# Filler matmuls moved to another PSUM bank, and loads of right sides pinned behind the output weights, in a fused attention and two-MoE kernel

## The chip, the cores and the metric

The kernel runs on one core of one Trainium2 chip. The metric is the device time of one execution in microseconds, smaller is better. A core has a matmul engine (TensorE, PE in the profile), a vector engine (DVE), a scalar engine (ACT), GpSimd (POOL) and a sync engine (SP). SP computes nothing here: nearly all DMAs are issued from its queue, in the order in which they stand there, and an issue that has to wait holds up every issue behind it.

## The reference

```python
def _attn_ref(q, k, v, tau):                      # (4, 8, 576, 64) each
    scores = scale * np.matmul(q, k.transpose(0, 1, 3, 2))
    thresh = np.max(scores, axis=-1, keepdims=True) - tau
    scores = np.where(scores >= thresh, scores, -1000000000.0)
    scores = scores - np.max(scores, axis=-1, keepdims=True)
    attn = np.exp(scores)
    attn = attn / (np.sum(attn, axis=-1, keepdims=True) + 1e-09)
    return np.matmul(attn, v)

def _moe_ref(x, w_in, w_out, s, b):               # x (2304, 512), w_in (512, 2048)
    r = np.maximum(x @ w_in, 0.0)
    return (s * (r * r) + b) @ w_out

def _moe2_ref(x, w_in, w_out):
    h = x @ w_in
    g = h * np.tanh(np.where(h > 20.0, h, np.log1p(np.exp(np.minimum(h, 20.0)))))
    return g @ w_out
```

The attention output, laid out as 2304 rows of 512, goes through the first layer pair (`_moe_ref`) and then the second (`_moe2_ref`).

## The kernel before

All large matmuls work on float32 split into two parts (high and low), so a product of two matrices is three matmuls.

**Attention.** The 32 heads are taken as 16 pairs `pr`; each pair has 9 score tiles `ti` of 128 rows by 576 columns, and the loop in `attention` counts them as `k = 9 * pr + ti`. For a tile, `scores` writes S into PSUM in two halves of 288 columns (line 318), one half in each bank of a two-bank tile. In the first three pairs it then writes two filler matmuls (`busy`, line 179: ones times ones, a result that nobody uses) into columns 800 to 1023 of the same tile (line 320). The fillers keep the matmul engine occupied. DVE then reads S (`ns`, line 324), ACT takes the exponential (line 331), DVE masks and sums (line 335), POOL normalizes (line 345). Seven tiles later `weights_t` transposes the weights into the PSUM tile `T` (lines 357 to 366) and ACT copies them out (`te`, line 368); `product` multiplies them with the values into the PSUM tile `pv` (line 379). The right order of all this is found by a scheduler that simulates a time line when the kernel is built, so the program's order on an engine isn't the order of the code.

PSUM has eight banks, and in the first stage four two-bank tiles fill them: two for S (also used for the transposed q and k, `tp`), one for `T`, one for `pv`. The transposed k of the next pair is made in tile 2 of a pair, q in tile 4: `raw_t` transposes, ACT copies the high part (`hik`, `hiq`, line 258), DVE subtracts (`lok`, `loq`, line 259), SP moves the parts into place (`KH`, line 279). The high part has one buffer, so `hiq` waits until `hik` has been moved.

Before the first tile, 16 wider fillers run in a tile called `warm`, which lies in the bank of `T` (lines 411 to 413).

**First layer pair.** `moe1` is interleaved with the attention from the time the first four pairs are there.

**Second layer pair.** `moe2` takes three blocks `sb` of 768 rows, with Strassen's scheme: seven products p = 1, 6, 5, 2, 7, 3, 4 in place of eight. For a block, `hidden` runs over j = 0 to 7; for each j it needs 7 weight parts in two tiles, `wi{sb}_{j}_0` (parts 6, 5, 1; 768 KB) and `wi{sb}_{j}_3` (parts 2, 4, 7, 3; 1024 KB), and seven right sides `yc{sb}_{p}`. A product is 6 matmuls (line 587). Then `output` runs over p = 1, 6, 2, 7, 5, 4, 3, each with 72 matmuls (line 721) and two weight tiles `wo{sb}_{p}_{q}` of 1024 KB (line 715). All `wi` and `wo` tiles share one ring of five buffers (`wr`): each load waits until the tile five places before it is done with. At the end of each p the output stage also asks for the right side of the same p for the next block (line 727), which the hidden stage has by then done with, and after the last three products and p = 2 it stores output tiles (line 671). The right sides of the next block are computed during `hidden` and stored to DRAM as `ycd` (line 559).

Of the kernel before, what the change touches and what calls it, by code (L numbers as in the profile page):

```python
# [8 lines left out]
F32 = mybir.dt.float32  # L9
# [6 lines left out]
P = 128  # L16
# [3 lines left out]
class Fused:  # L20
# [281 lines left out]
    def scores(self, pr, ti):  # L302
        nc = self.nc
        Q, KH, KL, E4 = self.sets[pr % 2]
        if ti == 0:
            self.st = self.at.tile([P, 5, 9], F32, tag="stat", name=f"st{pr}", bufs=2)
        st = self.st
        nm, nthr, sm, u, rinv = (st[:, i, :] for i in range(5))
        hs = [0] if ti < 4 else [1] if ti > 4 else [0, 1]
        cols = slice(512, 640) if ti == 4 else slice((ti % 5) * 128, (ti % 5) * 128 + 128)  # L310
        S = self.s_tile(f"S{pr}_{ti}")
        for hf in range(2):
            ks = slice(hf * 288, hf * 288 + 288)
            so = S[:, hf * HB:hf * HB + 288]
            terms = [(h, K[h]) for h in hs for K in (KH, KL)]
            for i, (h, kt) in enumerate(terms):
                c0 = ti * 128 + 64 * h if ti <= 4 else 64 + ti * 128
                nc.tensor.matmul(so, Q[:, c0:c0 + 128], kt[:, ks], start=(i == 0), stop=(i == len(terms) - 1))  # L318
        if pr < 3:
            self.busy(S[:, 800:1024], 2)  # L320
        ns = self.at.tile([P, 576], F32, tag="ns", name=f"ns{pr}_{ti}", bufs=2)
        sv = S.rearrange("p (h n) -> p h n", h=2)[:, :, :288]
        c1 = slice(ti, ti + 1)
        nc.vector.tensor_scalar(ns.rearrange("p (h n) -> p h n", h=2), sv, -0.125, 3.0e38,  # L324
                                op0=ALU.mult, op1=ALU.min, accum_out=nm[:, c1])
        nc.gpsimd.tensor_scalar(nthr[:, c1], nm[:, c1], self.tau_c, None, op0=ALU.add)  # L326

        if ti < 4:
            self.es[pr, ti, "pair"] = self.at.tile([P, 1152], F32, tag="e", name=f"e{pr}_{ti}", bufs=8)
        e = E4[:, 64:640] if ti == 4 else self.es[pr, ti % 5, "pair"][:, 0 if ti < 4 else 576:][:, :576]  # L330
        nc.scalar.activation(e, ns, AF.Exp, bias=nm[:, c1], scale=-1.0)  # L331
        self.es[pr, ti] = e

        def finish():
            nc.vector.scalar_tensor_tensor(e, ns, nthr[:, c1], e, op0=ALU.is_le, op1=ALU.mult, accum_out=sm[:, c1])  # L335
            if ti not in (1, 4, 8):
                return
            g = slice({1: 0, 4: 2, 8: 5}[ti], ti + 1)
            nc.vector.tensor_scalar(rinv[:, g], sm[:, g], 1.0e-9, None, op0=ALU.add)
            nc.vector.reciprocal(rinv[:, g], rinv[:, g])  # L340

            nc.vector.tensor_scalar(u[:, g], sm[:, g], 0.5, 1.0 / self.S, op0=ALU.is_lt, op1=ALU.mult)
            for j in range(g.start, g.stop):
                t = self.es[pr, j]
                nc.gpsimd.tensor_scalar(t, t, rinv[:, j:j + 1], u[:, j:j + 1], op0=ALU.mult, op1=ALU.add)  # L345

        return finish
# [49 lines left out]
    def attention(self):  # L397

        nc = self.nc
        N = 9 * self.B * self.NP
        LAG = 7
        for n in "kq":
            self.load_raw(0, n)
        nc.sync.dma_start(self.tau_c, self.tau.partition_broadcast(P))
        nc.sync.dma_start(self.s_c, self.s.partition_broadcast(P))
        nc.sync.dma_start(self.b_c, self.b.partition_broadcast(P))
        for pr in range(2):
            self.load_raw(pr, "v")  # L410
        warm = self.tp.tile([P, 1024], F32, tag="T", name="warm")
        self.busy(warm[:, :512], 10)
        self.prep_first(lambda n: self.busy(warm[:, :512], n))
        fin = todo = None
        tes = {}
        for k in range(N + LAG + 2):
            pr, ti = divmod(k, 9)
            if k < N:
                nxt = self.scores(pr, ti)
                if fin:  # L420
                    fin()
                fin = nxt
                yield 550
                if pr + 1 < self.B * self.NP and ti in (2, 4):
                    self.prep_qk(pr + 1, "kq"[ti // 2 - 1])
                    yield 500
            elif fin:
                fin()
                fin = None
            j = k - LAG  # L430
            if 0 <= j < N:
                prj, ci = divmod(j, 9)
                tnew = self.weights_t(prj, ci)
                yield 550
            if todo:
                tp, tc, te = todo
                tes[tc] = te
                if tc == 4:
                    self.product(tp, 4, (te, te), True, False)
                    yield 490  # L440
                elif tc > 4:
                    self.product(tp, tc - 5, (tes[tc - 5], te), False, tc == 8)
                    yield 970
                if tc == 8:
                    self.split_x(tp)
                    self.load_raw(tp + 2, "v")
            todo = (prj, ci, tnew) if 0 <= j < N else None
# [187 lines left out]
    def output(self, sb):  # L635
        nc = self.nc
# [69 lines left out]
        def run():  # L706
            for i, (p, q) in enumerate(seq):
# [16 lines left out]
                            after(p, t)  # L724
                if sb < 2 and q == 3:
                    t = self.yc[p] = self.ycp.tile([P, 2, 2, N2], F32R, tag=f"yc{p}", name=f"yc{sb + 1}_{p}")
                    nc.sync.dma_start(t.bitcast(F32), self.ycd[p])

        return prep, run

# [179 lines left out]
```

## Time and profile before

| what | value |
|---|---|
| three timed runs | 1165.19, 1164.51, 1174.03 us; median 1165.19 us |
| the profiled execution | 1174.32 us, of which the span of its instructions is 1172.3 us |
| PE busy | 1110.8 us (95% of the span) |
| mean granted TensorE clock | 0.983 |
| DMA | 292.71 MB, mean 250 GB/s |
| PE time in `output` (line 721) | 180.6 us, idle before it 5.3 us |

The profile is of one execution. Busy time of PE says only that a matmul was in the pipe. The granted clock is 1.00 where the engine runs at 2.4 GHz and 0.50 where it runs at 1.2 GHz; a figure between is a mean over a stretch that has both.

### The profile page before, as it was taken

The numbers are of one execution on the slowest core, as the hardware profiler recorded it, in microseconds if no ns is written. First come the engines' busy times: TensorE is split into PE (matmuls) and PEld (weight loads), VectorE is DVE, ScalarE is ACT, GpSimd is POOL, SyncE is SP. The second block draws the span as 40 slices with busy tenths as digits, with TensorE's granted clock in tenths as the row PEclk, the third lists the DMA queues.
The fourth block names the chain that finished last, engine by engine and source line by source line (L and its number), as shares of the span: only waits on it lengthen the run. The fifth ranks groups of instructions, "written<-read, shape, count | busy, mean of one in ns | idle before, by whom it ended". The sixth has DMA issues, their size and how long they took to land.

```text
span 1172.3 us, 21473 instructions
## 1 busy us (share of the span) xinstructions
PE 1110.8 (95%) x7966; PEld 1022.7 (87%) x7966; DVE 760.7 (65%) x1516; ACT 616.5 (53%) x1153; POOL 421.1 (36%) x536
## 2 busy tenths in 40 slices
PE   7888999998989989999899999999998999999998
PEld 5766788787788878888799889999998999999998
DVE  5678766869687575767676515573786368734783
ACT  4456675746557555557565447563453144513451
POOL 4457656658456565638475323310000000000000
PEclk8899999899999999999999999999998999999999
DMA  6347665675778778798876249998999899987783
GB/s 157 72 100 209 163 185 169 201 215 182 231 243 268 239 225 266 250 273 262 273 234 201 86 135 327 380 352 316 367 371 372 285 401 349 419 274 255 266 293 121
DMA packets 141592, 292.71 MB, mean 250 GB/s; under 512 B 52848, under 2 KB 78960, under 8 KB 133168
## 3 DMA queue, kind: packets, MB, share of 16 engines
q1 hardware_dynamic: 134256, 286.91, 73.1%
q10 hardware_dynamic: 7232, 4.43, 1.5%
q8 instruction: 63, 1.03, 0.4%
q14 instruction: 41, 0.34, 0.1%
HBM read 201.85 MB, written 66.58 MB: 229 GB/s over the span
## 4 chain that ended last, share of the span: by engine, by line
PE 55%; DMA 16%; DVE 12%; POOL 5%; ACT 5%; issue 5%; SPq 2%; ACTq 0%; DVEq 0%; POOLq 0%
PE o L721 13%; PE y L476 10%; PE h L476 8%; PE qY L587 6%; PE qX L587 4%; PE qV L587 4%; PE pv L379 4%; DVE e L335 3%; PE S L318 3%; DMA wo<-wso 3%; DMA crawi<-in_moe_w_in_dram 2%; POOL e L345 2%; PE T L357 2%; DMA wso<-chlo 2%; DMA wraw<-in_moe_w_in_dram 2%
## 5 line engine op out<-in xcount | busy, mean ns | idle before, releaser
L721 PE MATMUL o<-wo,hl 128*128 128x256 f32 x1512 | 180.6, 282 | 5.3 <-DMA wo<-wso 5.3
L721 PEld LDWEIGHTS o<-wo,hl 128*128 128x128 f32 x1512 | 180.1, 190 | 5.6 <-issue 3.6
L476 PE MATMUL y<-gh,w 128*128 128x288 f32 x768 | 165.2, 301 | 3.7 <-ACT y L521 2.4
L476 PE MATMUL h<-xh,w 128*128 128x288 f32 x768 | 163.9, 299 | 4.5 <-ACT r L497 2.1
L335 DVE SCALAR_TENSOR_TENSOR e<-ns,st,e 128x576 f32<-128x576 f32 x128 | 123.6, 970 | 61.6 <-ACT e L331 40.4
L324 DVE TENSOR_SCALAR_CACHE_REDUCE ns<-S 128x576 f32<-128x576 f32 x144 | 107.8, 753 | 58.1 <-PE S L318 46.8
L345 POOL TENSOR_SCALAR e<-e,st 128x576 f32<-128x576 f32 x128 | 133.1, 1049 | 32.8 <-DVE st L340 26.0
L476 PEld LDWEIGHTS y<-gh,w 128*128 128x128 f32 x768 | 126.9, 190 | 11.7 <-issue 6.6
L476 PEld LDWEIGHTS h<-xh,w 128*128 128x128 f32 x768 | 125.4, 188 | 12.8 <-issue 4.4
L368 ACT COPY te<-T 128x576 f32<-128x576 f32 x144 | 91.3, 634 | 76.5 <-PE T L362 70.5
L331 ACT ACTIVATE e<-ns,st 128x576 f32<-128x576 f32 x128 | 98.7, 778 | 58.1 <-DVE ns L324 55.4
L357 PE MATMUL T<-ident,e 128*128 128x128 f32 x576 | 98.2, 280 | 17.8 <-ACT te L368 10.2
L476 PE MATMUL y<-gl,w 128*128 128x288 f32 x384 | 114.2, 298 | 0.0
L476 PE MATMUL h<-xl,w 128*128 128x288 f32 x384 | 113.9, 297 | 0.0
L318 PE MATMUL S<-KH,Q 128*128 128x288 f32 x320 | 100.5, 330 | 14.1 <-DVE ns L324 9.1
L500 POOL TENSOR_TENSOR gl<-rr,gh 128x288 fp32r<-128x288 f32 x96 | 88.7, 927 | 68.8 <-ACT rr L499 68.6
L326 POOL TENSOR_SCALAR st<-st,small 128x1 f32<-128x1 f32 x144 | 62.0, 431 | 136.1 <-DVE ns L324 100.4
L379 PE MATMUL pv<-te,rawv 128*64 128x288 f32 x640 | 97.4, 421 | 0.0
L357 PEld LDWEIGHTS T<-ident,e 128*128 128x128 f32 x576 | 71.8, 145 | 26.0 <-ACT te L368 13.6
L318 PE MATMUL S<-KL,Q 128*128 128x288 f32 x320 | 93.2, 306 | 0.0
L318 PEld LDWEIGHTS S<-KH,Q 128*128 128x128 f32 x320 | 63.2, 198 | 28.0 <-DVE ns L324 14.3
L587 PE MATMUL qY<-yc,wi 128*128 128x384 f32 x432 | 86.6, 336 | 0.0
(147 smaller groups left out, 2296.8 us busy)
## 6 DMA issues: line engine op xcount, KB each, us to landing
w<-w SPq DMA_DIRECT2D x96, 512.0 KB, 5.2
wo<-wso SPq DMA_DIRECT2D x42, 1024.0 KB, 7.3
wi<-wsi SPq DMA_DIRECT2D x23, 1024.0 KB, 7.0
wi<-wsi SPq DMA_DIRECT2D x25, 768.0 KB, 5.9
w<-wp SPq DMA_DIRECT2D x32, 512.0 KB, 3.3
wsi<-chli SPq DMA_DIRECT2D x24, 512.0 KB, 4.5
wso<-chlo SPq DMA_DIRECT2D x24, 512.0 KB, 6.9
ycd<-yp SPq DMA_DIRECT2D x14, 768.0 KB, 6.1
```

The costliest lines, as they stand in the source:

```text
L318: nc.tensor.matmul(so, Q[:, c0:c0 + 128], kt[:, ks], start=(i == 0), stop=(i == len(terms) - 1))
L324: nc.vector.tensor_scalar(ns.rearrange("p (h n) -> p h n", h=2), sv, -0.125, 3.0e38, op0=ALU.mult, op1=ALU.min, accum_out=nm[:, c1])
L331: nc.scalar.activation(e, ns, AF.Exp, bias=nm[:, c1], scale=-1.0)
L335: nc.vector.scalar_tensor_tensor(e, ns, nthr[:, c1], e, op0=ALU.is_le, op1=ALU.mult, accum_out=sm[:, c1])
L345: nc.gpsimd.tensor_scalar(t, t, rinv[:, j:j + 1], u[:, j:j + 1], op0=ALU.mult, op1=ALU.add)
L357: nc.tensor.transpose(T[:, i * 128:i * 128 + 128], self.es[pr, i, "pair"][:, o:o + 128], self.ident)
L368: nc.scalar.copy(te, T[:, :576])
L379: return self.nc.tensor.matmul(self.pv[HALVES[h], hf * HB:hf * HB + 288], v[:, h, c, :], tes[h][:, hf * 288:hf * 288 + 288], start=first, ...
L476: nc.tensor.matmul(acc[:, :n], w[:, wl, c], rhs[c][xl][:, ts], start=(i == 0), stop=(i == 11))
L500: (nc.vector if b == 3 else nc.gpsimd).tensor_tensor(gl[:, ts], r2, gh[:, ts].bitcast(F32), op=ALU.subtract)
L587: self.nc.tensor.matmul(acc, a, b, start=(first and i == 0), stop=(i == n - 1), skip_group_check=True)
L721: nc.tensor.matmul(bank[p][t], hl[:, gl, j, ts], w[:, 2 * (q % 2) + j, wl], start=(old is None and q + j + k == 0), stop=(q + j + k == 6), ...
```

## The change

1. The fillers after each score tile no longer write into the S tile. They write 256 columns of `warm`, three at a time instead of two of 224 columns, after the first 12 tiles (k = 0 to 11) instead of the first 27 (three pairs).
2. `warm` is taken from the pool of `pv` instead of the pool of `T`. The first product of weights and values comes at k = 12 or later, so the bank is free until then.
3. The load of a right side for the next block (line 727) may no longer be moved ahead of earlier instructions of its queue: `keep_in_program_order` holds it behind everything that the code writes before it on SP.

```diff
--- before.py
+++ after.py
@@ -316,8 +316,6 @@
                 nc.tensor.matmul(so, Q[:, c0:c0 + 128], kt[:, ks], start=(i == 0), stop=(i == len(terms) - 1))
-        if pr < 3:
-            self.busy(S[:, 800:1024], 2)
         ns = self.at.tile([P, 576], F32, tag="ns", name=f"ns{pr}_{ti}", bufs=2)
@@ -408,15 +406,17 @@
-        warm = self.tp.tile([P, 1024], F32, tag="T", name="warm")
-        self.busy(warm[:, :512], 10)
-        self.prep_first(lambda n: self.busy(warm[:, :512], n))
+        warm = self.pvp.tile([P, 1024], F32, tag="pv", name="warm")[:, :512]
+        self.busy(warm, 10)
+        self.prep_first(lambda n: self.busy(warm, n))
         fin = todo = None
@@
             if k < N:
                 nxt = self.scores(pr, ti)
+                if k < 12:
+                    self.busy(warm[:, :256], 3)
                 if fin:
@@ -724,7 +724,7 @@
                     t = self.yc[p] = self.ycp.tile([P, 2, 2, N2], F32R, tag=f"yc{p}", name=f"yc{sb + 1}_{p}")
-                    nc.sync.dma_start(t.bitcast(F32), self.ycd[p])
+                    self.tc.keep_in_program_order(nc.sync.dma_start(t.bitcast(F32), self.ycd[p]))
```

The scheduler then places the instructions anew. Three places show it. In the names the last number counts allocations, and the numbers before it are those of the words above (`S0_1` is tile 1 of pair 0, `yc1_3` the right side p = 3 of block 1).

PE at the first two score tiles, before:

```order
L318 MATMUL S0_0_206<-KH00_119,Q0_117 128x288
L318 MATMUL S0_0_206<-KL00_121,Q0_117 128x288
L179 MATMUL S0_0_206<-ones_70 128x224 x2
L318 MATMUL S0_1_218<-KL00_121,Q0_117 128x288
L318 MATMUL S0_1_218<-KH00_119,Q0_117 128x288
L318 MATMUL S0_1_218<-KL00_121,Q0_117 128x288
L179 MATMUL S0_1_218<-ones_70 128x224 x2
```

PE at the same place now:

```order
L318 MATMUL S0_0_206<-KH00_119,Q0_117 128x288
L318 MATMUL S0_0_206<-KL00_121,Q0_117 128x288
L179 MATMUL warm_152<-ones_70 128x256 x3
L318 MATMUL S0_1_219<-KL00_121,Q0_117 128x288
L318 MATMUL S0_1_219<-KH00_119,Q0_117 128x288
L318 MATMUL S0_1_219<-KL00_121,Q0_117 128x288
L179 MATMUL warm_152<-ones_70 128x256 x3
```

The fillers stand where they stood, but no longer write what DVE reads next. From tile `S1_3` on there are none.

SP's queue in the output stage of block 0, before:

```order
L727 DMA yc1_6_10707<-ycd1_6_10087 128x1536
L715 DMA wo0_6_0_10618<-wso_66 128x2048
L727 DMA yc1_5_11010<-ycd1_5_10154 128x1536
L715 DMA wo0_6_2_10662<-wso_66 128x2048
L727 DMA yc1_2_10814<-ycd1_2_10223 128x1536
L727 DMA yc1_7_10908<-ycd1_7_10292 128x1536
L727 DMA yc1_3_11203<-ycd1_3_10361 128x1536
L715 DMA wo0_2_0_10714<-wso_66 128x2048
L715 DMA wo0_2_2_10762<-wso_66 128x2048
L727 DMA yc1_4_11116<-ycd1_4_10430 128x1536
L715 DMA wo0_7_0_10819<-wso_66 128x2048
```

SP's queue at the same place now:

```order
L715 DMA wo0_6_0_10600<-wso_66 128x2048
L715 DMA wo0_6_2_10644<-wso_66 128x2048
L727 DMA yc1_6_10689<-ycd1_6_10069 128x1536
L715 DMA wo0_2_0_10696<-wso_66 128x2048
L715 DMA wo0_2_2_10744<-wso_66 128x2048
L715 DMA wo0_7_0_10801<-wso_66 128x2048
L715 DMA wo0_7_2_10845<-wso_66 128x2048
L727 DMA yc1_7_10890<-ycd1_7_10274 128x1536
L715 DMA wo0_5_0_10898<-wso_66 128x2048
L715 DMA wo0_5_2_10942<-wso_66 128x2048
```

Four right sides (p = 5, 2, 7, 3) that stood ahead of the output weights `wo0_2` now stand behind them, and so does p = 4; p = 2, 5, 4 and 3 come later still than the rows shown, each behind the output stores of the same product. The same holds in block 1.

SP's queue at the end of that stage now, where the last right side stands:

```order
L671 DMA out_0_dram<-o0_011_11176 128x256
L593 DMA wi1_2_0_11336<-wsi_65 128x1536
L559 DMA ycd2_1_11264<-yp2_1_11261 128x1536
L671 DMA out_0_dram<-o0_012_11182 128x256
L727 DMA yc1_3_11185<-ycd1_3_10343 128x1536
L593 DMA wi1_2_3_11338<-wsi_65 128x2048
L593 DMA wi1_3_0_11406<-wsi_65 128x1536
L559 DMA ycd2_6_11334<-yp2_6_11331 128x1536
L593 DMA wi1_3_3_11408<-wsi_65 128x2048
L559 DMA ycd2_5_11401<-yp2_5_11398 128x1536
L559 DMA ycd2_2_11470<-yp2_2_11467 128x1536
L593 DMA wi1_4_0_11472<-wsi_65 128x1536
```

PE in the hidden stage of block 1 now, from its 14th product on:

```order
L587 MATMUL qV1_2_11343<-yc1_5_10992,wi1_2_0_11336 128x384 x6
L587 MATMUL qY1_1_11271<-yc1_4_11098,wi1_1_3_11268 128x384 x6
L587 MATMUL qV1_0_11194<-yc1_3_11185,wi1_0_3_11189 128x384 x6
L587 MATMUL qV1_1_11272<-yc1_3_11185,wi1_1_3_11268 128x384 x6
L587 MATMUL qX1_2_11341<-yc1_2_10796,wi1_2_3_11338 128x384 x6
L587 MATMUL qY1_2_11342<-yc1_7_10890,wi1_2_3_11338 128x384 x6
L587 MATMUL qV1_2_11343<-yc1_3_11185,wi1_2_3_11338 128x384 x6
L587 MATMUL qX1_3_11410<-yc1_1_10592,wi1_3_0_11406 128x384 x6
```

The scheduler has put the first product with `yc1_3` at place 16 of the stage (before: place 9), and it is the last that reads `wi1_0_3` (before: a product at place 11).

## Rows read from the trace of the kernel before

**Rows 1.** The page: the span, then busy time, share and instructions of PE.

```profile
span 1172.3 us, 21473 instructions
PE 1110.8 (95%) x7966; PEld 1022.7 (87%) x7966; DVE 760.7 (65%) x1516; ACT 616.5 (53%) x1153; POOL 421.1 (36%) x536
```

**Rows 2.** Who PE waited for, whole span: us in total, times, longest.

```profile
PE S L318 <- DVE ns L324: 9.1, 12, 1.4
PE o L721 <- DMA wo<-wso: 5.3, 2, 3.4
```

**Rows 3.** Stretches: start:end, us, busy of each engine (count), PEclk, DMA, GB/s.

```profile
24.00:36.00 12.00, 10.07 (x41) 9.18 (x42) 7.80 (x24) 5.21 (x8) 3.99 (x7) 0.50 0.22 50
...
48.00:60.00 12.00, 12.00 (x88) 8.08 (x87) 8.42 (x27) 6.94 (x12) 4.73 (x8) 1.00 0.24 53
...
84.00:96.00 12.00, 10.29 (x80) 8.17 (x78) 9.06 (x26) 7.29 (x13) 10.38 (x12) 1.00 0.54 124
...
108.00:120.00 12.00, 9.40 (x71) 7.47 (x69) 11.61 (x32) 8.47 (x14) 9.46 (x12) 1.00 0.69 184
...
888.00:900.00 12.00, 12.00 (x83) 12.00 (x83) 4.72 (x7) 4.20 (x7) 0.00 (x0) 0.77 0.98 400
900.00:912.00 12.00, 12.00 (x106) 12.00 (x105) 6.75 (x9) 4.68 (x7) 0.00 (x0) 1.00 0.86 293
...
948.00:960.00 12.00, 12.00 (x71) 12.00 (x71) 8.35 (x14) 3.51 (x8) 0.00 (x0) 1.00 1.00 384
```

**Rows 4.** PE's time line, output stages: start, us, ..., [idle before <-releaser].

```profile
887.74 4.61 PE L721 MATMUL o<-wo,hl 128*128 128x256 f32 x20 [3.44 <-DMA wo<-wso]
...
1009.50 2.69 PE L721 MATMUL o<-wo,hl 128*128 128x256 f32 x21 [1.87 <-DMA wo<-wso]
```

**Rows 5.** SP's time line, blocks 0 and 1: start, us, line, DMA, count.

```profile
865.50 3.80 SPq L727 DMA_DIRECT2D yc<-ycd  x3
870.85 2.13 SPq L715 DMA_DIRECT2D wo<-wso  x2
...
932.35 2.46 SPq L671 DMA_DIRECT2D out_dram<-o  x3
934.90 8.42 SPq L593 DMA_DIRECT2D wi<-wsi  x4
...
950.11 0.32 SPq L593 DMA_DIRECT2D wi<-wsi  x1
...
994.95 0.80 SPq L715 DMA_DIRECT2D wo<-wso  x2
```

**Rows 6.** DMA: 866 to 878, the page, 945 to 960, 1056 to 1068 (last: landing).

```profile
DMA packets 829, 5.07 MB, mean 422 GB/s; under 512 B 89, under 2 KB 89, under 8 KB 575
...
wo<-wso SPq DMA_DIRECT2D x42, 1024.0 KB, 7.3
...
wi<-wsi SPq DMA_DIRECT2D x2, 768.0 KB, 8.4
...
wi<-wsi SPq DMA_DIRECT2D x1, 768.0 KB, 4.1
```

**Rows 7.** The chain of waits by line, from 45 to 81 us.

```profile
by line: PE S L318 19.6%; PE pv L379 19.3%; DMA KH<-hik 11.7%; DVE e L335 8.7%; PE T L357 8.5%; issue 7.3%; PE S L179 6.9%; ACT te L368 3.2%; SPq L279 2.3%; DVE lok L259 1.9%; ACT hiq L258 1.9%; PE T L362 1.8%; ACT hik L258 1.7%; PE T L366 
```

**Rows 8.** Pieces of the chain from 0 to 135 us: start, us, what.

```profile
26.12 0.41 PE S L179 x2
...
50.00 0.21 PE S L179 x2
...
67.00 4.22 DMA KH<-hik
```

**Rows 9.** Who DVE waited for, 0 to 81 us.

```profile
DVE ns L324 <- PE S L179: 10.5, 9, 2.0
```

**Rows 10.** PE's time line at the start of block 1's hidden stage.

```profile
932.40 1.22 PE L587 MATMUL qX<-yc,wi 128*128 128x384 f32 x6
933.45 1.20 PE L587 MATMUL qY<-yc,wi 128*128 128x384 f32 x6
```

## The prediction

> **What bounds the kernel now.** I read the totals first: PE is busy for 95% of the span [rows 1]. So the change can win where PE stands idle, where it does work that nobody uses, and where it runs at the lower clock. The list of whom PE waited for then says how much idle time this change can reach: 5.3 us in two waits of the output stage for its weights (wo), and 9.1 us of score tiles that wait for DVE to read the one before [rows 2]. The table of stretches says where the clock was low: 0.50 from 24 to 36 us, and 0.77 right behind the first of the two waits; elsewhere in it 1.00 [rows 3].
>
> The two waits have one cause. In block 0 PE stands still for 3.44 us until 887.74, in block 1 for 1.87 us until 1009.50 [rows 4]. SP issued three right sides (yc) from 865.50 on, just ahead of the two wo loads of 870.85 [rows 5], and over 866 to 878 the DMA engines moved 422 GB/s [rows 6], the highest rate in any of these rows: they are full. The wo tiles are 1024 KB, the yc tiles 768 KB. Four yc tiles that the next hidden stage reads, from 932.40 on [rows 10], stand in a full queue ahead of wo tiles that are needed next.
>
> **The sum**, against the profiled execution, 1174.3 us.
>
> *Output weights, -5.3 us.* Now only yc1_1 and yc1_6 stand ahead of wo0_2. Its buffer comes free as before, so it is again asked for at 870.85; with a common landing time of 7.3 us [rows 6] it is there at 878, and it is needed at 887.74 - 3.44 = 884.3. That leaves 6 us. In block 1: 994.95 [rows 5] + 7.3 = 1002, needed at 1007.6. Both waits go, 3.44 + 1.87 = 5.3 us. The bytes do not go away: they move to the later part of the output stage, where the engines have room (293 GB/s from 900 to 912 [rows 3]).
>
> *The clock behind the first wait, -2.6 us.* From 888 to 900 PE was busy throughout but got through 83 matmuls at a clock of 0.77, against 106 in the next 12 us at 1.00 [rows 3]. The missing 23 are 23 x 12 / 106 = 2.6 us. PE stood idle, then fell to 1.2 GHz; without the idle time I expect no fall. Between 0 (it falls for another reason) and 2.6, I take 2.6 for this execution.
>
> *Fillers from k = 12 on, -2.0 us.* There the chain of waits runs largely through PE: from 45 to 81 us, 6.9% of 36 us = 2.5 us of it are fillers [rows 7], 0.21 us a pair at the full clock [rows 8]. All of these go. Not all of it can be kept: the chain also passes through the move of the key parts, 4.22 us of DMA [rows 8], and what PE gains between the transposes of k and of q it spends waiting for that move. Between 0 and 2.5 us, I take 2.0, nearer the upper end since the chain already counts only what was on the path. Later PE is busy 95% of the time like everywhere [rows 1], so what is gained stays.
>
> *Fillers up to k = 11, 0.* They grow from 2 x 224 to 3 x 256 columns, a factor of 1.71: a pair of 0.21 us becomes 0.36, one of 0.41 us at the low clock [rows 8] becomes 0.70. So 12 tiles x 0.15 to 0.29 = 1.8 to 3.5 us more work on PE. Against that DVE no longer waits for them: it waited nine times for a tile's fillers [rows 9], and 0.21 to 0.41 us of each wait are the fillers themselves, so 1.9 to 3.7 us. Here PE mostly waits for DVE. I put the two against each other and take 0, with 3.5 us either way.
>
> *A new wait in block 1's hidden stage, +1.6 us.* Call E the end of block 0's output stage (932.40 in the trace, the start of the first hidden product [rows 10]). Products are 1.04 us apart [rows 10]. The output stores now hold yc1_3 back to about E + 2.5 (the three took from 932.35 to 934.8 [rows 5]). It lands by E + 11 even at the 8.4 us that a 768 KB load took in a full stretch [rows 6], and its first reader is the 16th product, at E + 15.6: in time. But that product is the last reader of wi1_0_3, and the ring has five buffers, so wi1_3_0 can be asked for only at E + 16.7, where the trace before has the same load between 934.90 and 943.3 [rows 5]. Everything behind it on SP stands still meanwhile. With 4.1 us for a 768 KB load in an empty queue [rows 6] it lands at E + 20.8, just when the 21st product wants it. Behind it come ycd2_6, wi1_3_3, ycd2_5, ycd2_2 and wi1_4_0: 4.2 MB, at 422 GB/s 10 us, so wi1_4_0 lands at E + 30.8, wanted by the 29th product at E + 29.1. That is a wait of about 1.7 us; I take 1.6. The lower end is 0, if the stores are slow to come and the weights pass. The upper end: wi1_3_0, wi1_3_3 and two stores, 3.4 MB or 8 us, are late in a stage whose DMA already moved 384 GB/s [rows 3]. Before, wi1_4_0 was asked for at 950.11 [rows 5], there at 958.5 and needed at 961.5, so 3 us to spare; 8 - 3 = 5 us. In block 2 nothing is stored for a next block, and a weight load took 4.1 us there [rows 6]: wi2_3_0, free after product 12 at E + 12.5, lands at E + 17 and is needed at E + 19.8. No wait.
>
> Moving `warm` to the bank of `pv` costs nothing: the first product that needs the bank comes on PE itself, behind the last filler.
>
> Sum: -5.3 - 2.6 - 2.0 + 0 + 1.6 = -8.3, so 1166.0 us for an execution like the profiled one. That one is 9.1 us over the median of the three runs; another of them, 1174.03, is as long, and the trace does not say which part of it the two shorter runs lack. The low clock behind the wait may be such a part. For the median I count half of it: 1165.2 - 5.3 - 1.3 - 2.0 + 1.6 = **1158.2 us**.
>
> **The clock and a rule against this change.** In the tiles k = 12 to 26 the fillers are gone while PE still makes the transposes (T). From 84 to 96 and from 108 to 120 us, where no fillers ran before either, the clock is 1.00 with PE busy 10.3 and 9.4 of 12 us and the same transposes [rows 3]. I take it that scores and products keep the clock up. The Trainium skill (TensorE: Matmul & The Clock Gate, Part 4: PE-mode transpose) says that transposes do not count as PE work for the full clock in the way that other matmuls do. By that, tiles with fewer real matmuls would fall to the low clock; the two stretches here do not show it.
>
> **Rivals.**
>
> *The clock falls where the fillers are taken away* (10%). From 48 to 60 us PE did 88 matmuls in 12.0 us at 1.00; from 24 to 36 us 41 in 10.07 us at 0.50 [rows 3]: 0.136 against 0.246 us, a factor of 1.8. The 36 us from 45 to 81 hold at most 33.5 us of PE work without fillers; at the low clock they take 27 us more at most, and half of that if the clock falls for half of them. 1158 + 13 = 1171 us, above 1177 if it lasts. It decides once it costs 7 us, that is from some 16 us of PE time at the low clock on (16 x 0.8 / 1.8 = 7); then the kernel is slower than before. For it: 0.50 from 24 to 36 us although fillers ran. Against it: the stretches without fillers.
>
> *The wider fillers hold the clock up early* (16%). The stretch at 0.50 has 41 matmuls in 10.07 us; at 0.136 us they take 5.6. Up to 4.5 us, and 1 to 2 more around it: 1152 to 1154 us. Against it: PE there also waits for moves and for DVE, which fillers right behind a tile do not fill.
>
> *The fillers were hidden anyway* (14%): the moves and DVE set the pace, the 2.0 us do not come. 1160 us, or 1163 if the wider fillers cost what they add.
>
> *The late weights cost their upper end* (15%): 5 in place of 1.6 us, and the queue recovers late. 1162 to 1165 us.
>
> My forecast (45%) lies between 1153 and 1162.
>
> **Range and chances.** 1148 to 1169 us: it takes in the forecast with its bounds, both cases near it and the early clock; it leaves out most of the fall of the clock. A measurement of this kernel can tell about 1% from no change, which is 11.7 us: faster means below 1153.5, slower above 1176.8. Faster: two thirds of the early clock and a fifth of the forecast (where the low clock behind the wait was in the median runs too), 0.11 + 0.09, and a little for what I have not seen: 0.22. Slower: half of the fall of the clock, 0.05. The same: 0.73.
>
> **What would show it.** PE's two waits for wo are gone and the time from the first to the last matmul of block 0's output stage is 3.4 us or more shorter; the clock from 888 to 900 is 1.00. A wait of the hidden stage for wi some 17 to 31 us after its start in block 1, of 0 to 5 us, none in block 2. DVE's waits for fillers are gone, and the first product of the first layer pair starts about 2 us earlier, with a clock from 45 to 81 us no lower than before. I am wrong if the wo loads still come late (then yc was not what delayed them), if the hidden stage of block 1 waits over 5 us, or if the stretch from 45 to 81 us is longer with a lower clock.

## The result and the profile after

| what | before | after |
|---|---|---|
| median of 14 runs each | 1171.05 us | 1158.78 us (1153.39 to 1165.72) |
| ratio to before, 95% interval | | 0.9894 [0.9868, 0.9921] |
| the profiled execution | 1174.32 us | 1162.64 us |
| its span | 1172.3 us | 1160.7 us |
| its mean granted clock | 0.983 | 0.988 |

The change makes the kernel about 1.1% faster. The forecast of 1158 us lies within 1 us of the median. It was worked out from the three runs of before that were known, with a median of 1165.19 us; over 14 runs before has 1171.05 us. The forecast gain was 7.0 us, the measured one is 12.3 us, so the terms of the sum were too small together. The experiments show where.

The page of the changed kernel: the span, then busy time, share and instructions of each engine [rows 1].

```profile
span 1160.7 us, 21427 instructions
PE 1106.9 (95%) x7948; PEld 1017.5 (88%) x7948; DVE 757.5 (65%) x1516; ACT 618.2 (53%) x1153; POOL 420.1 (36%) x536
```

PE has 18 matmuls less: 54 fillers of 224 columns have become 36 of 256. The span is 11.6 us shorter, but PE's busy time only 3.9 us: most of the gain is not work that was saved.

Who PE waited for in the changed kernel, whole span: us in total, times, longest [rows 2].

```profile
PE S L318 <- DVE ns L322: 7.5, 12, 1.3
...
PE qY L587 <- DVE g L610: 1.3, 2, 0.7
...
PE qX L587 <- DMA wi<-wsi: 0.6, 1, 0.6
```

The 5.3 us for wo are gone without a remainder; three short waits in the hidden stages stand in their place, 1.9 us together.

PE's time line of the changed kernel: start, us, the work, and in brackets the idle time before it with its releaser [rows 4, 10].

```profile
124.86 0.40 PE L476 MATMUL h<-xh,wp 128*128 128x288 f32 x1
...
798.80 1.31 PE L587 MATMUL qX<-yc,wi 128*128 128x384 f32 x6 [0.61 <-DVE y L523]
...
856.12 3.43 PE L721 MATMUL o<-wo,hl 128*128 128x256 f32 x28
...
915.96 1.20 PE L587 MATMUL qX<-yc,wi 128*128 128x384 f32 x6
...
921.98 1.32 PE L587 MATMUL qY<-yc,wi 128*128 128x384 f32 x6 [0.65 <-DVE g L610]
...
947.07 1.32 PE L587 MATMUL qX<-yc,wi 128*128 128x384 f32 x6 [0.61 <-DMA wi<-wsi]
948.23 1.21 PE L587 MATMUL qY<-yc,wi 128*128 128x384 f32 x6
949.27 1.22 PE L587 MATMUL qV<-yc,wi 128*128 128x384 f32 x6
950.33 1.37 PE L587 MATMUL qX<-yc,wi 128*128 128x384 f32 x6
951.52 1.37 PE L587 MATMUL qY<-yc,wi 128*128 128x384 f32 x6
...
1044.99 1.32 PE L587 MATMUL qY<-yc,wi 128*128 128x384 f32 x6 [0.65 <-DVE g L610]
```

Block 0's output stage lasts from its first matmul at 856.12 to the first hidden product of block 1 at 915.96, which is 59.84 us. PE's time line before has these rows for the first layer pair, the second one and the output stage, which ended at 932.40 [rows 10]:

```profile
131.59 0.40 PE L476 MATMUL h<-xh,wp 128*128 128x288 f32 x1
...
808.98 1.31 PE L587 MATMUL qX<-yc,wi 128*128 128x384 f32 x6 [0.61 <-DVE y L523]
...
866.29 3.43 PE L721 MATMUL o<-wo,hl 128*128 128x256 f32 x28
```

From 866.29 that is 66.11 us, so the stretch lost 6.27 us: the wait of 3.44 us [rows 4] and 2.8 us in which the clock had been low. In the hidden stage of block 1 PE waits at 921.98 for DVE (g), which has to read a bank before the next product may be written there, and at 947.07 for weights. From 950.33 on, products follow each other every 1.20 us instead of 1.04; the last section comes back to that.

Stretches of the changed kernel: start:end, us, busy of PE, PEld, DVE, ACT and POOL (counts), granted clock, DMA share, GB/s [rows 3].

```profile
24.00:36.00 12.00, 10.11 (x65) 8.96 (x63) 8.08 (x27) 6.48 (x10) 4.88 (x11) 0.86 0.18 41
45.00:81.00 36.00, 31.08 (x217) 22.49 (x212) 26.29 (x74) 20.02 (x32) 17.10 (x26) 0.95 0.41 99
60.00:72.00 12.00, 7.79 (x49) 5.80 (x50) 7.61 (x23) 4.78 (x8) 5.66 (x8) 0.88 0.77 175
888.00:900.00 12.00, 12.00 (x106) 12.00 (x105) 7.29 (x12) 4.82 (x6) 0.00 (x0) 1.00 0.91 343
950.00:979.00 29.00, 29.00 (x147) 27.87 (x146) 19.98 (x31) 11.77 (x20) 0.00 (x0) 1.00 0.94 356
```

From 24 to 36 us PE gets through 65 matmuls at a mean clock of 0.86, against 41 at 0.50. From 888 to 900 the clock is 1.00 and the count 106, against 0.77 and 83. From 45 to 81 us, where most of the fillers are gone, the clock is 0.95; the same stretch before:

```profile
45.00:81.00 36.00, 32.34 (x226) 25.68 (x225) 23.63 (x67) 19.37 (x30) 17.20 (x26) 0.93 0.49 113
```

Whom DVE waited for in the changed kernel, 0 to 81 us [rows 9]:

```profile
DVE lok L259 <- ACT hik L258: 6.9, 2, 6.4
DVE ns L322 <- PE S L318: 6.5, 6, 1.6
```

No wait for fillers is left. DVE now waits for the scores themselves, 6.5 us in six times against 10.5 us in nine. Of those nine, before, only two lie in the first 12 tiles, whose last filler starts at 36.14 us; the other seven come after 45 us. DVE's waits for fillers before, from 0 to 45 and from 45 to 81 us:

```profile
DVE ns L324 <- PE S L179: 2.1, 2, 1.3
DVE ns L324 <- PE S L179: 8.4, 7, 2.0
```

SP's time line of the changed kernel at the start of block 1: start, us, line, DMA, count [rows 5].

```profile
919.93 0.32 SPq L727 DMA_DIRECT2D yc<-ycd  x1
921.94 4.83 SPq L593 DMA_DIRECT2D wi<-wsi  x2
930.76 0.32 SPq L559 DMA_DIRECT2D ycd<-yp  x1
931.65 0.32 SPq L593 DMA_DIRECT2D wi<-wsi  x1
932.02 1.67 SPq L559 DMA_DIRECT2D ycd<-yp  x2
933.78 1.31 SPq L593 DMA_DIRECT2D wi<-wsi  x2
```

In the order of the queue these are yc1_3; wi1_2_3 and wi1_3_0; ycd2_6; wi1_3_3; ycd2_5 and ycd2_2; wi1_4_0 and wi1_4_3. The DMA view of the stretch from 933.7 to 934.2 us holds wi1_4_0 alone (last: us from issue to landing):

```profile
wi<-wsi SPq DMA_DIRECT2D x1, 768.0 KB, 13.2
```

933.78 + 13.2 = 947.0: the load of 768 KB that takes 4.1 us in an empty queue [rows 6] takes 13.2 us here, and PE's wait ends with it at 947.07.

### The profile page after: what moved, and what is told of

Read it like the earlier page. It is cut to its first block, busy times and chain, and to the rows that moved or that the text cites. A ratio compares the mean times of both kernels' runs of the same rounds, so it can differ in the third digit from the quotient of the medians.

```text
span 1160.7 us, 21427 instructions
## 1 busy us (share of the span) xinstructions
PE 1106.9 (95%) x7948; PEld 1017.5 (88%) x7948; DVE 757.5 (65%) x1516; ACT 618.2 (53%) x1153; POOL 420.1 (36%) x536
## 4 chain that ended last, share of the span: by engine, by line
PE 57%; DMA 14%; DVE 10%; issue 7%; POOL 6%; ACT 5%; SPq 2%; ACTq 0%; POOLq 0%; DVEq 0%
PE o L721 15%; PE h L476 8%; PE y L476 7%; PE qY L587 6%; PE pv L377 5%; PE qX L587 4%; PE qV L587 4%; PE S L318 4%; DMA wso<-chlo 3%; PE T L355 3%; DVE e L333 3%; POOL e L343 2%; DMA wraw<-in_moe_w_in_dram 2%; DMA wraw<-in_moe_w_out_dram 2%; DMA w<-w 2%
## 5 line engine op out<-in xcount | busy, mean ns | idle before, releaser
L721 PE MATMUL o<-wo,hl 128*128 128x256 f32 x1512 | 177.7, 279 | 0.0
L721 PEld LDWEIGHTS o<-wo,hl 128*128 128x128 f32 x1512 | 177.4, 188 | 0.0
L476 PEld LDWEIGHTS h<-xh,w 128*128 128x128 f32 x768 | 126.8, 190 | 12.6 <-issue 4.6
L476 PEld LDWEIGHTS y<-gh,w 128*128 128x128 f32 x768 | 125.8, 188 | 8.9 <-issue 6.6
```

The source lines that it names most:

```text
L476: nc.tensor.matmul(acc[:, :n], w[:, wl, c], rhs[c][xl][:, ts], start=(i == 0), stop=(i == 11))
L721: nc.tensor.matmul(bank[p][t], hl[:, gl, j, ts], w[:, 2 * (q % 2) + j, wl], start=(old is None and q + j + k == 0), stop=(q + j + k == 6), ...
```

## Experiments

Theory: the pinned loads give what the sum says of the output stage (the two waits and the clock, less a new wait), and the rest comes from the fillers. Rivals: one of the halves does nothing; the fillers' place, number or width matters by the clock; the whole difference is scatter between executions. All ratios are to the kernel before, run beside them; its median was 1170.34 us beside the first four kernels, 1168.17 us beside the next four and 1167.77 us beside the last three. The us behind a ratio are worked out from the ratio; they differ by up to 1.5 us from the difference of the two medians.

**The change once more**, unaltered.

> The changed kernel once more, beside its two halves. Both theories: about 0.989 of the kernel before. What its trace tells apart: in the first trace of the change the products of block 1's hidden stage ran at 1.20 us each instead of 1.04 from 950 us on, 28 us long, at a granted clock of 1.00, and lost 4 us. If the new order of loads does that, the slow products are here again at the same place; if it is chance, block 1's hidden stage takes about 59 us here.

Measured: 1157.58 us, 0.9904 [0.9869, 0.9939], span of the profiled execution 1152.5 us. The result stands. The waits are the same (0.65 us at 917.42, 0.83 us for wi at 942.68, 0.65 us at 1036.76). The slow products are not here: block 1's hidden stage takes 59.5 us (911.41 to 970.87) against 63.2 us (915.96 to 979.11), so they do not come from the order of the loads alone. The span is 8.2 us shorter than that of the first profile of the same program, so a single span says little about a few us.

**The pinned loads alone**: the kernel before with

```diff
-                    nc.sync.dma_start(t.bitcast(F32), self.ycd[p])
+                    self.tc.keep_in_program_order(nc.sync.dma_start(t.bitcast(F32), self.ycd[p]))
```

> The kernel before with the loads of right sides pinned and nothing else. Theory A (the two waits for output weights are the larger part): both waits gone, no low clock behind the first, waits of about 0.6 us for wi and 1.3 us for DVE in the hidden stages as in the change: 4 to 7 us less, a ratio of 0.994 to 0.9965. Rival B (most of the change comes from the fillers): the bytes only move, 0 to 3 us, a ratio of 0.9975 to 1.000. The first product of the first layer pair at 131 to 132 us as before by both.

Measured: 1163.32 us, 0.9945 [0.9921, 0.9969], or -6.4 us. PE's time line of this kernel:

```profile
127.86 0.40 PE L476 MATMUL h<-xh,wp 128*128 128x288 f32 x1
...
803.62 1.31 PE L587 MATMUL qX<-yc,wi 128*128 128x384 f32 x6 [0.61 <-DVE y L523]
...
860.94 3.43 PE L721 MATMUL o<-wo,hl 128*128 128x256 f32 x28
...
926.80 1.32 PE L587 MATMUL qY<-yc,wi 128*128 128x384 f32 x6 [0.65 <-DVE g L610]
...
954.90 1.29 PE L587 MATMUL qX<-yc,wi 128*128 128x384 f32 x6 [0.77 <-DMA wi<-wsi]
```

No wait for wo, and two of the three short waits. Up to the first output stage this program has the same instructions in the same order as the kernel before. Yet its first product of the first layer pair starts at 127.86 us and that of the second pair at 803.62, against 131.59 and 808.98 before: 5.4 us that come from nothing in the order of the program. From this point to the end, before took 1172.3 - 809.0 = 363.3 us, this kernel 1160.6 - 803.6 = 357.0: -6.3 us, which is what the ratio says too.

**The fillers alone**: the changed kernel with the load as before.

```diff
-                    self.tc.keep_in_program_order(nc.sync.dma_start(t.bitcast(F32), self.ycd[p]))
+                    nc.sync.dma_start(t.bitcast(F32), self.ycd[p])
```

> The change with the loads of right sides left free: the fillers' half alone. Theory A: the first stage 2 to 4 us shorter, both waits for output weights as before (5.3 us), a ratio of 0.9965 to 0.998. Rival B: the first product of the first layer pair at about 125 us, 6 to 7 us earlier, a ratio of 0.994 to 0.995, with less time at the low clock before 45 us.

Measured: 1161.82 us, 0.9940 [0.9914, 0.9965], or -7.0 us. That is rival B, with the first product of the first layer pair at 125.81 us. The waits for wo are back (3.15 and 2.33 us). The halves multiply to 0.9945 x 0.9940 = 0.9885, and the whole was 0.9894: they add up. So 7.0 us [4.1, 10.1] is what the fillers' part brings, and my sum had 2.0 for it.

**No fillers behind the score tiles at all**: the kernel before without them.

```diff
-        if pr < 3:
-            self.busy(S[:, 800:1024], 2)
```

> The kernel before without any filler after a score tile (the 16 before the first tile stay). If fillers keep the clock up in the first stage, it falls to 0.5 for longer between 12 and 80 us and the first product of the first layer pair comes later than at 131.6 us, by 3 to 15 us: a ratio of 1.003 to 1.013. If they are only work that nobody uses, the first stage is 2 to 4 us shorter: 0.9965 to 0.998, as in the fillers' half alone, and then it is not where they write that matters.

Measured: 1160.48 us, 0.9921 [0.9895, 0.9947], or -9.2 us, below both forecasts. The fillers that the change keeps, and the new bank of `warm` (it lies in the bank of `T` here), are not needed for the gain; leaving the fillers out does at least as much. Stretches of this kernel:

```profile
24.00:36.00 12.00, 8.88 (x45) 7.39 (x43) 10.66 (x36) 6.42 (x10) 8.40 (x12) 0.72 0.20 46
36.00:48.00 12.00, 10.01 (x76) 8.00 (x78) 8.40 (x22) 6.47 (x11) 7.83 (x11) 1.00 0.76 173
48.00:60.00 12.00, 10.94 (x83) 8.32 (x80) 10.31 (x29) 8.20 (x13) 5.38 (x10) 1.00 0.21 52
60.00:72.00 12.00, 9.65 (x61) 6.70 (x60) 7.62 (x23) 5.93 (x10) 7.04 (x10) 0.86 0.81 192
879.00:891.00 12.00, 12.00 (x82) 12.00 (x83) 4.52 (x7) 4.09 (x7) 0.00 (x0) 0.77 0.95 380
```

Without a filler the clock from 24 to 36 us is 0.72, and that from 36 to 60 is 1.00; before it was 0.50 and, from 48, 1.00 [rows 3]. DVE is busy 10.66 of the 12 us with 36 instructions, against 7.80 and 24: DVE gets further here, at whatever clock PE has. The last row stands behind the wait of block 0's output stage, as [rows 3] from 888 us; PE's time line of this kernel has that wait:

```profile
878.81 45.19 PE L719 MATMUL o<-wo,hl 128*128 128x256 f32 x360 [3.70 <-DMA wo<-wso]
```

3.70 us idle, then a clock of 0.77 again. The last section has all such waits.

**Fewer fillers, old width, in the new bank**: the fillers' part of the change, load as before, two of 224 columns.

```diff
-                    self.busy(warm[:, :256], 3)
+                    self.busy(warm[:, :224], 2)
```

> The fillers' half alone, but 2 x 224 columns as before, in the bank of the first product, for k = 0 to 11; loads of right sides left free. If what counts is that DVE no longer waits for a filler, the ratio is that of the fillers' half, 0.994, or a little below. If what counts is how many fillers there are, it lies between that and the kernel without any (0.992): 0.992 to 0.994. If the wider fillers are what helped (through the clock), it is back near 0.997.

Measured: 1165.60 us, 0.9971 [0.9948, 0.9993], or -3.4 us. By the ratio that is the third case, the width.

**Fewer fillers, old width, in the old place**: the kernel before with

```diff
-        if pr < 3:
+        if pr * 9 + ti < 12:
```

> The kernel before with its fillers (2 x 224 columns in the score tile) for k = 0 to 11 only, none in the 15 tiles after. If the gain of the fillers' half is the 15 tiles without fillers, the ratio is 0.994 to 0.996. If it is the bank, 0.998 to 1.000.

Measured: 1165.35 us, 0.9977 [0.9959, 0.9994], or -2.7 us. This is the term "from k = 12 on" by itself; the sum had -2.0. By the ratios the new bank adds 0.7 us to it, by the medians nothing; both are within the scatter. By the ratios what is left to the 7.0 us comes with the greater width: 0.9971 to 0.9940, whose intervals still overlap. The traces share it out otherwise: the first product of the first layer pair starts at 128.5 us with these fillers, at 125.9 with the same ones in the new bank, and at 124.5 to 126.8 with the wide ones, so there it is the bank. Which of the two it is stays open. From 24 to 36 us the stretch of the new bank with narrow fillers, of the old place with narrow fillers (each in a fence of its own) and that of the changed kernel above are:

```profile
24.00:36.00 12.00, 10.14 (x59) 9.00 (x59) 8.13 (x26) 5.92 (x10) 4.05 (x10) 0.75 0.11 26
```

```profile
24.00:36.00 12.00, 9.51 (x50) 8.18 (x51) 8.55 (x27) 5.55 (x10) 4.18 (x8) 0.75 0.22 50
```

The clock is 0.75, 0.75 and 0.86. The higher clock goes with the width, but 12 us at 0.86 in place of 0.75 are 1.3 us, not 3.6.

**No fillers and the pinned loads**, both edits above on the kernel before.

> No fillers after score tiles, and the loads of right sides pinned. If the parts add, 0.992 x 0.9945 = 0.9865, some 3 us below the change, whose ratio is 0.989 to 0.990. If the fillers that the change kept are worth their time, it is no faster than the change: 0.989 or above.

Measured: 1153.71 us, 0.9871 [0.9846, 0.9897]: the product of its parts is 0.9921 x 0.9945 = 0.9866. By the medians it is faster than the change, but the intervals overlap.

**No fillers, and the pinned load written earlier**: between the two weight loads of its own product, not behind it.

```diff
+                if sb < 2 and q == 1:
+                    t = self.yc[p] = self.ycp.tile([P, 2, 2, N2], F32R, tag=f"yc{p}", name=f"yc{sb + 1}_{p}")
+                    self.tc.keep_in_program_order(nc.sync.dma_start(t.bitcast(F32), self.ycd[p]))
                 hl = ready.pop(i)
...
-                if sb < 2 and q == 3:
```

> As the kernel without fillers and with pinned loads, but each load of a right side is asked for between the two weight loads of its product, not behind its output stores. If the new small waits of the hidden stages (0.6 to 0.8 us for wi, 0.65 us twice for DVE) come from the last right sides being held behind stores, they are gone here: 1 to 2.5 us below the kernel without fillers and with pinned loads, a ratio of 0.984 to 0.986. If an early load hinders the output weights again, their waits come back and it is 0.988 or above.

Measured: 1148.08 us (1146.58 to 1150.06), 0.9833 [0.9807, 0.9859], faster than the kernel before and than the change. The one row that is left of PE's waits from 780 us to the end:

```profile
PE qX L585 <- DVE y L521: 0.6, 1, 0.6
```

Neither wo nor wi nor g is waited for. On PE's time line of this kernel the two marks stand at

```profile
120.87 0.40 PE L474 MATMUL h<-xh,wp 128*128 128x288 f32 x1
...
788.89 1.31 PE L585 MATMUL qX<-yc,wi 128*128 128x384 f32 x6 [0.61 <-DVE y L521]
```

and in the version before it, whose instructions are the same up to here, at

```profile
123.61 0.40 PE L474 MATMUL h<-xh,wp 128*128 128x288 f32 x1
...
795.82 1.31 PE L585 MATMUL qX<-yc,wi 128*128 128x384 f32 x6 [0.61 <-DVE y L521]
```

From there to the end it is 1144.6 - 788.9 = 355.7 against 1152.5 - 795.8 = 356.7 us. So the earlier place is worth 1.0 us by the profiles, the waits it removes. The medians of the two differ by 5.6 us, and their runs do not overlap (1150.09 to 1154.57 us in the version before). So the other 4.6 us are no scatter of single executions; the edit does not explain them, and the profiles have them ahead of it.

**The change with the early load**, fillers kept.

> The changed kernel, its fillers kept, with the pinned load of a right side written between the two weight loads of its own product instead of behind that product. Theory 1 (the place of the load and the fillers are separate prices): the change, 0.990 of the kernel before, times what the early place was worth without fillers (0.9833 / 0.9871 = 0.996), so about 0.986 or 1152 us, and no wait of the hidden stage for weights of block 1. Rival (the early place pays only where no fillers run, because the kernel without fillers reaches the output stage at another time): 0.990, as the change. Rival 2 (the short fillers cost nothing, the whole lead of the version without fillers was the early place): 0.983, as that version.

Measured: 1155.41 us, 0.9890 [0.9864, 0.9916]. The waits of the hidden stages are gone here too, and from the mark to the end it takes 1152.5 - 797.4 = 355.1 us, 3.1 less than the change in its second profile (358.2). The ratio fits the first rival (0.990); 0.986 lies just outside the interval, and 0.983 is excluded: the lead of the version without fillers is not the early place alone.

**Twice the fillers** in the changed kernel.

```diff
-                    self.busy(warm[:, :256], 3)
+                    self.busy(warm[:, :256], 6)
```

> The changed kernel with twice the fillers: six of 256 columns in place of three behind each of the first 12 tiles, 36 more of 0.11 us at the full clock, 3.9 us of added PE work. Theory 1 (fillers in the bank that nobody waits for are work on PE's path, and do not set the clock): 2 to 4 us longer than the change, 0.992 to 0.993 of the kernel before, and the clock from 24 to 36 us stays under 1.00. Rival (more fillers keep the clock up in the first 12 tiles): the clock from 24 to 36 us is 1.00 and the time is that of the change or less, 0.990 or lower.

Measured: 1157.75 us, 0.9921 [0.9893, 0.9949]. Its stretches:

```profile
12.00:24.00 12.00, 10.10 (x77) 9.14 (x75) 9.09 (x27) 5.50 (x8) 5.80 (x8) 1.00 0.83 189
24.00:36.00 12.00, 10.70 (x75) 10.47 (x76) 9.04 (x30) 5.50 (x9) 5.06 (x9) 0.86 0.22 50
```

The clock from 24 to 36 us stays at 0.86. The rival's sign (1.00, and 0.990 or less) did not come. The ratio is theory 1's, but 0.9921 is not apart from 0.9894 by the intervals, and the trace does not show the price where the fillers stand: the first product of the first layer pair starts at 125.2 us, against 124.9 and 124.5 in the change.

**The fastest version again**, beside these two.

> The version without fillers after the score tiles and with the early pinned load, once more, beside the two others on one chip: 0.983 of the kernel before, 1148 us, if its time holds on another chip; 0.987 if its lead over the pinned load at the old place was chance.

Measured: 1148.38 us, 0.9829 [0.9802, 0.9856]. It holds. Beside it the change with the early load, which differs in the fillers and the bank of `warm` alone, takes 7.0 us more. So the fillers that the change keeps cost 3 us (1157 against 1153.7 with the pinned load, whose intervals overlap) to 7 us against none; since two kernels with the same instructions up to the output stage came out 4.6 us apart above, this figure is no better known than that.

The profiled executions by part, in us (the two marks are read as in the rows above, the clock from the stretch up to the first):

| fillers, loads | first layer pair starts | mean clock until then | from there to the second pair | from there to the end |
|---|---|---|---|---|
| before, free | 131.6 | 0.91 | 677.4 | 363.3 |
| before, pinned | 127.9 | 0.93 | 675.8 | 357.0 |
| before, but k = 0 to 11 only, free | 128.5 | 0.92 | 671.5 | 363.1 |
| changed, but 2 of 224, free | 125.9 | 0.93 | 670.8 | 362.5 |
| changed, free | 125.8 | 0.95 | 670.8 | 364.2 |
| changed, pinned (two executions) | 124.9, 124.5 | 0.96, 0.97 | 673.9, 669.8 | 361.9, 358.2 |
| changed, pinned early | 126.8 | 0.93 | 670.6 | 355.1 |
| doubled, pinned | 125.2 | 0.96 | 676.9 | 358.2 |
| none, free | 123.5 | 0.94 | 676.3 | 365.8 |
| none, pinned | 123.6 | 0.92 | 672.2 | 356.7 |
| none, pinned early (two executions) | 120.9, 121.9 | 0.96, 0.93 | 668.0, 669.1 | 355.7, 355.7 |

The last column goes by the loads alone: 362 to 366 us free, 357 to 358 pinned, 355 to 356 early (361.9 is the execution with the slow products). The first goes by the fillers: mean 129.7 with those of before, 125.5 with the changed ones, 122.5 with none, and no execution without fillers is as late as one with the changed ones. It does not go by the clock: at a mean of 0.93 it is 127.9, 125.9, 126.8 and 121.9, at 0.96 it is 124.9, 125.2 and 120.9. The middle column scatters by 2 to 8 us within one kind of fillers, although between kinds at most 45 of PE's 4,424 matmuls there stand at another place. Its clock is 0.99 to 1.00 throughout (1.00 in the execution with 675.8), so the clock does not explain the scatter.

The first tiles in the same 13 executions, in the order of the table:

| fillers in the first 12 tiles | clock 12 to 24 us | clock 24 to 36 us | DVE's instructions 24 to 36 us |
|---|---|---|---|
| 2 of 224, in the score tile | 0.96, 1.00, 0.97 | 0.50, 0.72, 0.75 | 24, 25, 27 |
| 2 of 224, new bank | 0.97 | 0.75 | 26 |
| 3 of 256, new bank | 1.00 in all four | 0.86 in all four | 29, 27, 29, 29 |
| 6 of 256, new bank | 1.00 | 0.86 | 30 |
| none | 0.86, 0.86, 0.86, 0.90 | 0.72, 0.57, 0.72, 0.53 | 36, 36, 34, 34 |

With the wide fillers the clock is higher here than with the narrow ones, and without fillers it is lower still from 12 to 24 us. Yet DVE gets furthest without them.

## Why the prediction held, and where it did not

*Output weights, -5.3 us*: right. Both waits are gone in every kernel with pinned loads (3.44 + 1.87 us), and back in all four without them (5.5 to 6.3 us).

*The clock behind the first wait, -2.6 us*: right in kind, and in size for the profiled execution. Block 0's output stage is 6.27 us shorter, of which 3.44 is the wait, and every pinned execution has 59.8 us for it. Over the five profiled executions with that wait the clock behind it cost 0 to 3.0 us, 1.7 in the mean (last section), so the half that I took for the median, 1.3, was nearly right. What I put at nothing is the clock behind the second wait, in block 1: 0 in the execution that I read, 0.9 us in the mean of the five.

*The new wait in block 1*: +0.6 us against +1.6 forecast for the weights, at the very product that was named (wi1_4_0, the 29th). The load landed at 947.0, which is 31.0 us after the stage's start (915.96), against 30.8 forecast; the product wanted it at 30.5 (947.07 - 0.61), not at 29.1. That the landing fits to 0.2 us is luck, for the way there was another. The five buffers are not taken in turn, as I had it: in the program as built, wi1_3_0 follows wi1_1_0 in its buffer, and it is wi1_4_0 that follows wi1_0_3, whose last reader is the 16th product. The trace agrees. wi1_3_0 was asked for 10.5 us after the start (926.45 is the second of the two issues that end at 926.77), when the ninth product was done, not at 16.7, and took 10.1 us where I had 4.1 (the DMA view of its issue). wi1_4_0 was asked for at 933.78, 17.8 us after the start, when the 16th product, begun at 932.50, was done, and took 13.2 us in a full queue. What I missed is the product that now follows another into the same bank: qY with p = 4 stands right behind qY with p = 7 and waits 0.65 us for DVE, in block 1 and again in block 2, where I had written that there would be none. It was in the order of PE's instructions to be seen. All three cost 1.9 us, against 1.6 in the sum: one error made up for the other.

The pinned loads: -5.3 - 2.6 + 1.6 = -6.3 by the sum, -6.4 us measured alone. The terms fit the other executions too: over the five without pinned loads the two waits take 5.6 us and the clock behind them 2.5, the new waits of the pinned ones (the early load aside) are 1.1 to 2.4, and the last column of the table falls from a mean of 363.8 to 357.5 us (without the execution with the slow products). This half of the prediction is shown.

*Fillers from k = 12 on, -2.0 us*: -2.7 [-4.8, -0.7] measured alone. Right. Seven of DVE's nine waits for fillers belong here, 8.4 us, which the sum did not name; in the execution of the pinned loads, with the same instructions, it was three waits of 4.2 us together from 45 us on.

*Fillers up to k = 11, 0*: this is the weak step. The fillers' part is worth 7.0 us [4.1, 10.1] and not 2.0; less the 2.7 above, some 4.3 us belong to the first 12 tiles, where I set the wider fillers against DVE's waits and took zero, with 3.5 us either way. 4.3 is beyond that, though not clear of the scatter of the two figures. The balance itself was misread: I set all nine of DVE's waits against these fillers, but only two of them, 2.1 us together, lie in the first 12 tiles. By the rule that I used, that takes 0.4 to 0.8 us off and not 1.9 to 3.7, against 1.8 to 3.5 us of added work, so the sum should have had a loss here. Nor did the added work cost what I set for it: with twice the fillers the first layer pair starts no later. And the cause of the gain in these tiles is not shown. The ratios give 3.6 of the 4.3 us to the width and 0.7 to the bank; the start of the first layer pair gives 0.4 to the width and 2.6 to the bank. What is shown is that fillers in these tiles have a price of their own, since with none at all the first layer pair starts 3.0 us earlier than with the changed ones, and 4 to 5 us earlier at the same mean clock.

*The rivals.* That the clock falls where fillers go did not happen from 45 to 81 us: 0.95 with the changed fillers and 0.95 to 1.00 with none, against 0.93 before and 1.00 in the other execution with the fillers of before. Where the kernels without fillers lack them in the first 12 tiles too, it is lower (0.86 to 0.90 from 12 to 24 us against 0.96 to 1.00), and they are faster all the same. That the wider fillers hold the clock up early did happen (0.86 from 24 to 36 us in five executions, 0.50 to 0.75 with the narrow ones), but at the first layer pair it does not show. The Trainium skill (TensorE: Matmul & The Clock Gate, Part 4: PE-mode transpose) states that PE-mode transposes do not count as PE work for the full clock as other matmuls do. From 60 to 72 us the clock was 0.88 with the changed fillers and 0.86 with none, against 1.00 before, which is 1.4 to 1.7 us; but the trace before has such a dip, 0.86, from 72 to 84, and the fastest version has 1.00 from 60 to 72 in one execution and 0.86 in the other. No run here shows more of that rule than this. That the fillers were hidden anyway is refuted by 0.9940. The late weights cost 0.6 to 0.8 us in the change and with the pinned loads alone, 1.0 with twice the fillers, not 5.

*The number.* 1158.2 was the sum for a base of 1165.2; on the base of 1171.05 it would have been 1164. That it lies within 1 us of the median is luck, from two errors that cancel: the three runs known before lay low in a range from 1164.5 to 1179.6 us, and the fillers were worth 5 us more.

What stays open: why executions of the same instructions differ by up to 11 us ahead of the second layer pair (788.9 to 799.8 with no fillers), and with it how much of the fillers' 7.0 us arises in the first 130 us (4.2 by the means of the table) and how much only later, where no filler stands; and whether it is the bank or the width of the fillers in the first 12 tiles that gains.

## What to carry to other kernels

In a stage whose DMA queue is full, a prefetch that stands ahead of an urgent load can cost the wait for that load, and a clock fall on top if the matmul engine goes idle: write the prefetch behind the urgent load, and as early after it as its buffer allows. Test filler matmuls against none before moving or widening them: here they kept the clock up and still cost time. And where a kernel scatters by 1%, compare stages between marks in the traces, since what lies ahead of an edit with the same instructions shows how large the scatter is; and when a balance is read from a count of waits, look where in the kernel each of them lies.

## What was not expected of the hardware

**Products at the full clock, but slower.** In the first profile of the change, 27 products or so from 950.33 to 979 us follow each other in 1.20 us, with a granted clock of 1.00 and 147 matmuls in 29 us. That is 5.1 a us. The second profile of the same program has 71 in 12 us of the same stage, 5.9 a us:

```profile
945.00:957.00 12.00, 12.00 (x71) 12.00 (x70) 7.87 (x13) 5.33 (x9) 0.00 (x0) 1.00 1.01 407
```

27 x 0.16 us = 4.3 us, which is the difference of 361.9 and 358.2 in the table within 0.6. Nothing in the profile names the cause.

**A short wait may or may not cost the clock.** Behind each wait for wo stand the same 360 matmuls of the output stage. At the full clock they take 42.24 us; what they take above that is the price of the low clock. Two of the first waits, with the change's fillers alone and with the old width in the new bank:

```profile
875.12 43.53 PE L721 MATMUL o<-wo,hl 128*128 128x256 f32 x360 [3.15 <-DMA wo<-wso]
874.63 42.24 PE L721 MATMUL o<-wo,hl 128*128 128x256 f32 x360 [2.63 <-DMA wo<-wso]
```

All ten such waits in the five kernels with free loads, by length, in us:

| wait | 1.87 | 2.07 | 2.33 | 2.58 | 2.63 | 2.82 | 3.15 | 3.44 | 3.60 | 3.70 |
|---|---|---|---|---|---|---|---|---|---|---|
| block | 1 | 1 | 1 | 1 | 0 | 1 | 0 | 0 | 0 | 0 |
| above 42.24 | 0 | 0.40 | 1.92 | 0.40 | 0 | 1.56 | 1.29 | 2.58 | 1.56 | 2.95 |

The longer waits cost more in the mean, but a wait of 2.33 us cost 1.92 and one of 2.63 nothing. So the price of a single wait can't be read off its length here, and one execution is not enough to know it.
